# Cosine attention and a gated layer on one core: one quad's transposes, the order of the loads, one multiply, the last store, and the planner's transfer times

## Chip, core and metric

The kernel runs on one core of a Trainium2 chip. The metric is the device time of one execution in microseconds. It is measured in several runs, of which the median is given, and one further execution is recorded by the hardware profiler. All lines L... are lines of the kernel before.

## What is computed

For 8 batches and 12 heads, with 448 tokens and 64 elements a head, the rows of q and k are divided by their norms, and softmax(q k^T / 0.1) v is formed. The heads of a token then stand side by side, 768 wide, and pass through two dense layers with h cos(h) between them.

```python
q_n = q / (np.linalg.norm(q, axis=-1, keepdims=True) + 1e-06)
k_n = k / (np.linalg.norm(k, axis=-1, keepdims=True) + 1e-06)
scores = np.matmul(q_n, k_n.transpose(0, 1, 3, 2)) / tau          # tau = 0.1
attn = softmax(scores);  attn_out = np.matmul(attn, v)
x = attn_out.transpose(0, 2, 1, 3).reshape(B * S, H * D)          # 3584 x 768
h = x @ w_in                                                      # 768 x 2048
out = (h * np.cos(h)) @ w_out                                     # 2048 x 768
```

## The kernel before, in words

**Quads.** The work of the attention is cut into 24 quads of four heads, three for each batch (quad = 3 batch + 0, 1, 2). For a quad the kernel does the following.

- It loads q and k from DRAM as f32 into one of three buffers `Qf` and `Kf` (`load_qk`, L401, two DMAs issued by SyncE) and v into one of four (`load_v`, a DMA of GpSimd's queue).
- It squares them (`square`, L450, on GpSimd from quad 3 on) and sums the squares (L454, VectorE). Both stand in `norm_a`.
- It forms the inverse norms (`inverse`, L480 to L493, ScalarE and for some quads VectorE) and scales q and k to bf16 tiles `Qn` and `Kn` (`scale`, L501, GpSimd from quad 3 on). Both stand in `norm_b`.
- It transposes `Qn` and `Kn` to `qT` and `kT`. There are two ways. `transpose` (L516) lets TensorE transpose seven 128x128 blocks into a PSUM bank (L523), and VectorE copies the bank to `qT` or `kT` (L534); quads 0 to 2 use it. `turn` (L539) issues two DMA transposes on SyncE (L544); quads 3 to 23 use it.
- For each of seven steps it forms the scores (`scores`, L560, four matmuls), and ScalarE takes their exponential from two PSUM banks into a tile `E` (L567); `attend` (L577) multiplies `E` with v into banks 4 and 5. After the seventh step VectorE copies these banks to `AVs` (L586).
- It forms the sums of the softmax. For quads 0 to 2 this is done on the chip (`spread`, L599). From quad 3 on `sums` (L642) does it for one or two quads at a time: 14 matmuls a quad, a logarithm and an exponential on ScalarE (L649, L651), a DMA of the inverses to a DRAM tensor `rscr` issued by ScalarE (L652), two DMAs on SyncE for each quad that read them back, spread over the partitions, as `R` (L658), and a multiply of `AVs` with `R` into the bf16 tile `xT` (L661, GpSimd).

**Batches.** When the three quads of a batch are in `xT`, the first layer runs (`m1_part`, L675: 96 matmuls in eight pairs of blocks of 128), with the cosine behind it: two passes of ScalarE (L688, L692) and two of VectorE (L690, L694) for each pair, the last of which writes `gT`. The second layer (`m2`, L703) takes tiles of 128 tokens and the output's two halves of 384; each half is 16 matmuls. VectorE copies the half to `osb` (L711), and after the second half two DMAs on SyncE store the tile, 64 tokens each (L717).

**The order.** Quads 0 to 2 are done in a hand-written prologue. Then the loop over batches c = 0 to 7 does the first layer of batch c and interleaves the second layer of batch c with the quads that lie ahead: `QUADS = [5, 4, 3, 3, 3, 3, 0, 0]`, so quads 3 to 7 stand beside batch 0 and quads 8 to 11 beside batch 1. Before the first group of scores `fill(2 * E2)` puts 24 second-layer matmuls (L965). `group` (L745) takes two steps of a quad; at a quad's first step it calls `begin` (L739) and `norm_a` of the quad three ahead, and at its last step `turn` of the quad two ahead. `begin(qd)` loads q and k of quad qd + 4 and runs `norm_b` of quad qd + 2. Quad 3's turn is called right behind the prologue (L901).

**Engines and queues.** All instructions are objects of a `Planner` (class at the file's top). TensorE keeps the order in which the program made them. For ScalarE, VectorE, GpSimd and SyncE the planner simulates the run with the durations that each `op` is given, picks the next instruction of each engine by readiness and urgency, and so writes a fixed order for each engine before the run. A DMA is given the time `moves` that its transfer takes; `land` lets the transfers of a queue follow each other and slows them where two queues overlap. `lead` makes an instruction more urgent. Instructions made with `keep=True` keep their order among themselves on their engine. On SyncE these are the turns, and the loads of q and k of quads 5 and up; the loads of `R` and the stores are placed freely. At run time each engine works strictly in its order and waits for semaphores.

What a DMA issue looks like to the planner:

```python
o.lat = self.FIRST + moves + self.LAST if dma else self.LAT[eng]      # FIRST, LAST = 1.2, 0.8
```

## Time and profile before

| | |
|---|---|
| median of 3 runs | 444.45 us (443.76 to 445.1) |
| span of the profiled execution | 447.7 us; the page gives no other time for it |
| TensorE, matmul (PE) | 423.9 us busy, 95% of the span |
| ScalarE (ACT) | 315.3 us, 70% |
| VectorE (DVE) | 252.9 us, 56% |
| GpSimd (POOL) | 212.3 us, 47% |
| DMA queue of SyncE | 51.85 MB, 46.4% of 16 engines' span |
| DMA queue of GpSimd | 11.80 MB, 17.5% |

The profile is one execution, cut into instructions. A row of a timeline has the start, the length, the engine, the line, the operation, the tiles written and read, and in brackets the engine's idle time before it with the instruction that ended it. `PEld` is the load of weights into TensorE, which overlaps the matmuls. `SPq` is SyncE's own queue: issuing a DMA, not moving it. A row of the chain has start, length and what the end of the run was waiting for at that time. A row of stretches has the busy time of each engine, the clock granted to TensorE and the share in which the DMA engines were busy; the share can exceed 1 where packets of several queues overlap. Matmul records overlap by their pipelined ends, so the time of one matmul is read from a run of many.

### The profile page before, as it was taken

To read this page: it belongs to the slowest core of one execution; us is meant where nothing else is said; L and a number is where in the kernel's file an instruction comes from. 1 tells how busy PE (TensorE), PEld (TensorE's weight loads), DVE (VectorE), ACT (ScalarE), POOL (GpSimd) and SP (SyncE) were. 2 spreads that over 40 slices of the span, in tenths; PEclk is the share of its full clock that TensorE was granted. 3 is DMA by queue.
4 is the path that set the end of the run, shared out by engine and by line. 5 is a ranking of instruction groups with operands and counts; after the bars stand their busy time and mean duration, and the time that the engine had idled before them with its cause. 6 is when DMAs were issued, how large, how long until landed. Compare 5 with 4: busy or idle time off the path is not lost.

```text
span 447.7 us, 8380 instructions
## 1 busy us (share of the span) xinstructions
PE 423.9 (95%) x3530; PEld 206.4 (46%) x3530; DVE 252.9 (56%) x297; ACT 315.3 (70%) x434; POOL 212.3 (47%) x146
## 2 busy tenths in 40 slices
PE   7989978898999999999999999999999999999995
PEld 6444533233544445534454445534454445555553
DVE  4766974351894438935485348935484136825921
ACT  4898768785778887879678766879678666715700
POOL 3787618577628967069635682069232020030000
PEclk9999999988999999999999999999999999999999
DMA  7999998995917999159951996057811711051022
GB/s 248 237 256 222 221 233 106 272 205 139 252 23 152 265 182 253 29 132 250 171 154 39 240 210 170 1 130 191 164 38 35 162 40 34 0 156 35 1 70 72
DMA packets 72639, 64.81 MB, mean 145 GB/s; under 512 B 41924, under 2 KB 64792, under 8 KB 72600
## 3 DMA queue, kind: packets, MB, share of 16 engines
q1 hardware_dynamic: 59600, 51.85, 46.4%
q0 software_dynamic: 12288, 11.80, 17.5%
q8 instruction: 28, 0.46, 0.4%
q10 hardware_dynamic: 712, 0.61, 0.4%
q14 instruction: 11, 0.09, 0.1%
HBM read 55.25 MB, written 11.16 MB: 148 GB/s over the span
## 4 chain that ended last, share of the span: by engine, by line
PE 75%; DMA 13%; POOL 4%; ACT 3%; DVE 2%; issue 2%; SPq 1%; ACTq 0%; POOLq 0%
PE PS L703 30%; PE PS L675 29%; DMA Kf<-in_k_dram 8%; PE PS L560 6%; PE PS L577 5%; PE PS L642 3%; ACT E L567 2%; DMA kT<-Kn 2%; DMA R<-rscr 1%; DMA Qf<-in_q_dram 1%; POOL sqk L450 1%; DMA rscr<-Zs 1%; POOL Qn L501 1%; POOL Kn L501 1%; DVE n L454 1%
## 5 line engine op out<-in xcount | busy, mean ns | idle before, releaser
L567 ACT ACTIVATE E<-PS 128x896 bf16<-128x896 f32 x168 | 144.8, 916 | 30.3 <-PE PS L560 27.1
L703 PE MATMUL PS<-W,gT 128*128 128x384 bf16 x896 | 163.9, 328 | 1.8 <-DVE osb L711 1.0
L675 PE MATMUL PS<-xT,W 128*128 128x448 bf16 x768 | 149.2, 355 | 2.2 <-POOL xT L661 2.2
L703 PEld LDWEIGHTS PS<-W,gT 128*128 128x128 bf16 x896 | 80.2, 98 | 82.2 <-issue 28.8
L675 PEld LDWEIGHTS PS<-xT,W 128*128 128x128 bf16 x768 | 74.8, 98 | 73.9 <-issue 3.4
L688 ACT ACTIVATE ar<-PS 128x896 int32<-128x896 f32 x64 | 58.2, 911 | 51.1 <-PE PS L675 51.1
L690 DVE SCALAR_TENSOR_TENSOR ar<-ar,PS 128x896 f32<-128x896 int32 x64 | 69.2, 1083 | 32.2 <-ACT ar L688 32.2
L661 POOL TENSOR_TENSOR xT<-AVs,R 128x896 bf16<-128x896 f32 x21 | 43.5, 2085 | 87.8 <-DMA R<-rscr 87.8
L711 DVE COPY osb<-PS 128x384 f32<-128x384 f32 x56 | 30.2, 555 | 91.3 <-PE PS L703 91.3
L694 DVE TENSOR_TENSOR gT<-PS,ar 128x896 bf16<-128x896 f32 x64 | 69.6, 1088 | 1.5 <-ACT ar L692 1.0
L560 PE MATMUL PS<-qT,kT 64*64 64x448 bf16 x672 | 61.9, 367 | 8.7 <-DMA kT<-Kn 4.3
L692 ACT ACTIVATE ar<-ar 128x896 f32<-128x896 f32 x64 | 60.6, 946 | 12.9 <-DVE ar L690 12.9
L450 POOL TENSOR_TENSOR sqq<-Qf 128x896 bf16<-128x896 f32 x21 | 35.3, 1681 | 56.8 <-DVE n L454 36.8
L577 PE MATMUL PS<-E,Vb 64*64 64x448 bf16 x672 | 50.8, 354 | 1.6 <-ACT E L567 1.4
L450 POOL TENSOR_TENSOR sqk<-Kf 128x896 bf16<-128x896 f32 (+1 forms) x22 | 36.7, 1669 | 22.9 <-DVE n L454 12.9
L501 POOL TENSOR_TENSOR Qn<-Qf,rr 128x896 bf16<-128x896 f32 x21 | 35.5, 1690 | 14.6 <-ACT rr L493 14.5
L586 DVE COPY AVs<-PS 128x896 f32<-128x896 f32 x21 | 22.9, 1091 | 31.1 <-PE PS L577 31.1
L560 PEld LDWEIGHTS PS<-qT,kT 64*64 64x64 bf16 x672 | 18.6, 105 | 42.4 <-ACT E L567 15.8
L501 POOL TENSOR_TENSOR Kn<-Kf,rr 128x896 bf16<-128x896 f32 (+1 forms) x22 | 36.7, 1669 | 0.5 <-DVE Qn L501 0.5
L454 DVE TENSOR_REDUCE n<-sqk 128x14 f32<-128x896 bf16 (+2 forms) x24 | 25.0, 1040 | 8.0 <-POOL sqk L450 7.9
L454 DVE TENSOR_REDUCE n<-sqq 128x14 f32<-128x896 bf16 (+2 forms) x24 | 25.0, 1041 | 5.0 <-POOL sqq L450 4.5
L577 PEld LDWEIGHTS PS<-E,Vb 64*64 64x64 bf16 x672 | 19.4, 106 | 17.6 <-ACT E L567 10.5
(51 smaller groups left out, 174.1 us busy)
## 6 DMA issues: line engine op xcount, KB each, us to landing
Qf<-in_q_dram SPq DMA_DIRECT2D x24, 448.0 KB, 5.3
out_dram<-osb SPq DMA_DIRECT2D x56, 192.0 KB, 2.9
Kf<-in_k_dram SPq DMA_DIRECT2D x23, 448.0 KB, 5.9
R<-rscr SPq DMA_DIRECT2D x42, 224.0 KB, 4.6
Vb<-in_v_dram POOLq DMA_DIRECT2D x24, 224.0 KB, 5.6
W<-in_moe_w_in_dram POOLq DMA_DIRECT2D x4, 768.0 KB, 17.1
W<-in_moe_w_out_dram POOLq DMA_DIRECT2D x4, 768.0 KB, 29.7
qT<-Qn SPq DMA_TRANSPOSE x21, 4.5
```

The lines of the kernel that those rows point to most:

```text
L450: op(eng, (1.68 if eng == "pool" else 1.05) * n, lambda e: e.tensor_tensor(dst, src, src, ALU.mult), r=cut(nm + "f", s, part), w=at, after ...
L454: return op("dve", 0.07 + 0.95 * n, lambda e: e.tensor_reduce(out=n2[u].ap()[:, H * w:H * w + H] if part == ALL[0] else jr(n2[u], w, part) ...
L501: lambda e: e.tensor_tensor(n[u].ap()[:, j0:j1].rearrange("p j r d -> p r j d"), f[s].ap()[:, :, j0:j1], rb, ALU.mult),
L560: ins = e.matmul(bank(bs + r, S, 64 * a, 64 * a + 64), kT[u].ap()[64 * r:64 * r + 64, j, a, :], qT[u].ap()[64 * r:64 * r + 64, :, a, :], s ...
L567: act("exp", 0.875, lambda e: e.activation(E[es].ap(), two(bs), ACT.Exp, bias=0.0, scale=INV_TAU), r=pair(bs), w=[("E", es)], chain="E")
L577: ins = e.matmul(bank((X, Y)[a], S, 64 * r, 64 * r + 64), Vb[vs].ap()[64 * a:64 * a + 64, r, j, :], E[es].ap()[64 * a:64 * a + 64, r, :], ...
L675: ins = e.matmul(bank(bk + i2), W1.ap()[:, i, 128 * nb:128 * nb + 128], xT[c % 2].ap()[:, i, :], start=(i == 0), stop=(i == NKC - 1))
L688: op("act", 0.815, lambda e: e.activation(ar[s].ap().bitcast(I32), two(bk), ACT.Identity, bias=0.25, scale=INV2PI), r=bs, w=[("ar", s)])
L690: op("dve", 1.005, lambda e: e.scalar_tensor_tensor(ar[s].ap(), ar[s].ap().bitcast(I32), -2.0 * math.pi, two(bk), ALU.mult, ALU.add), r=bs ...
L692: act("sin", 0.86, lambda e: e.activation(ar[s].ap(), ar[s].ap(), ACT.Sin, bias=GUARD * math.pi / 2.0, scale=GUARD), r=[("ar", s)], w=[("a ...
L694: op("dve", 1.01, lambda e: e.tensor_tensor(gT.ap()[:, 2 * pr:2 * pr + 2, col:col + S], two(bk), ar[s].ap(), ALU.mult), r=bs + [("ar", s)] ...
L703: ins = e.matmul(bank(bk, HW), gT.ap()[:, f, col:col + 128], W2.ap()[:, f, HW * h:HW * h + HW], start=(f == 0), stop=(f == NNB - 1))
```

## The change

It has five parts.

- Quad 3 is transposed by TensorE. The call of `turn(FIRST)` behind the prologue goes; behind the first layer of batch 0 two calls of `transpose` come, into banks `free` and `free + 1` (2 and 3). In batch 0 the fill ahead of the first scores is 2 x E1 = 20 matmuls instead of 2 x E2 = 24.
- The loads of q and k of quad qd + 4 are made behind `turn(qd + 2)` at the quad's last step and no longer in `begin(qd)`. This holds for quads 8 to 23.
- The multiply that gives quad 5's x (the last of batch 1) is made on VectorE instead of GpSimd.
- The last output tile is stored in halves: each half of 384 columns gets its two DMAs as soon as it is copied, and of the second half one is issued by ScalarE.
- The transfer times that the planner is given are changed.

```diff
 load_one:    moves=0.17 * (j1 - j0)   ->  moves=0.196 * (j1 - j0)
 load_v:      moves=1.41  ->  1.67
 load_w1:     moves=4.15  ->  4.26
 load_w2:     moves=4.32  ->  5.18
 turn:        moves=1.2   ->  1.61
 R (L658):    moves=0.82  ->  0.85
 store (L717): moves=0.64 ->  0.66
@@ sums
-            op("pool", 2.04, lambda e, u=u, sl=sl, b=b, c0=c0: e.tensor_tensor(
+            late = qd == 2 * QB - 1
+            op("dve" if late else "pool", 1.02 if late else 2.04, lambda e, u=u, sl=sl, b=b, c0=c0: e.tensor_tensor(
                 xT[b % 2].ap()[:, c0:c0 + 2, :], AVs[sl].ap(), R[u].ap(), ALU.mult),
@@ m2
-        if f1 == NNB:
+        if f1 == NNB and t == B * S // 128 - 1:
+            so = t % 3
+            op("dve", 0.475, lambda e: e.tensor_copy(osb[so].ap()[:, HW * h:HW * h + HW], bank(bk, HW)),
+               r=whole(bk), w=[("o", so, h)])
+            for sg, eng in enumerate(("sp", "act" if h else "sp")):
+                b, cc = divmod(128 * t + 64 * sg, S)
+                dst = bass.AP(out.tensor, (S * b + cc // 64) * KM + HW * h, [[NJ * KM, 64], [1, HW]])
+                op(eng, 0.5, lambda e, sg=sg, dst=dst: e.dma_start(
+                    dst, osb[so].ap()[64 * sg:64 * sg + 64, HW * h:HW * h + HW]),
+                   r=[("o", so, h)], w=[("out", t, sg, h)], dma=("store", t, h, sg), moves=0.32)
+        elif f1 == NNB:
@@ begin
-        if FIRST < qd < NQ - 4:
-            load_qk(qd + 4)
         if FIRST < qd < NQ - 2:
             norm_b(qd + 2, after=[o for o in P.ops if o.chain][-1:])
@@ group
         if qd + 2 < NQ and j == NJ - 1:
             turn(qd + 2)
+            if FIRST < qd < NQ - 4:
+                load_qk(qd + 4)
@@ behind the prologue
     load_qk(FIRST + 3)
-    turn(FIRST)
     norm_b(FIRST + 1, after=ended[-1:])
@@ loop over batches, behind the first layer
         if c == 0:
+            transpose(FIRST, 0, free)
+            transpose(FIRST, 1, free + 1)
             norm_a(FIRST + 2, [o for o in P.ops if o.eng == "dve"][-1:])
@@
         if todo:
-            fill(2 * E2)
+            fill(2 * (E2 if c else E1))
```

More of the change, by code (lines that the diff above doesn't have):

```diff
@@ L398, in load_one @@
         return op(eng, 0.5, lambda e: e.dma_start(dst[s].ap()[:, :, j0:j1].rearrange("p r j d -> p r (j d)"), ap),
-                  w=cut(nm, s, part), dma=(nm, s, j0), moves=0.17 * (j1 - j0), after=after, keep=qd > 4)
+                  w=cut(nm, s, part), dma=(nm, s, j0), moves=0.196 * (j1 - j0), after=after, keep=qd > 4)
     def load_qk(qd, after=()):
@@ L410, in load_v @@
         return pool_dma(0.75, lambda e: e.dma_start(Vb[s].ap().rearrange("p r j d -> p r (j d)"), ap),
-                  w=[("V", s)], dma=("V", s), moves=1.41, after=after)
+                  w=[("V", s)], dma=("V", s), moves=1.67, after=after)
     NW = 2
@@ L717, in m2 @@
                     op("sp", 0.5, lambda e, sg=sg, dst=dst: e.dma_start(dst, osb[so].ap()[64 * sg:64 * sg + 64, :]),
-                       r=[("o", so, 0), ("o", so, 1)], w=[("out", t, sg)], dma=("store", so, sg), moves=0.64)
+                       r=[("o", so, 0), ("o", so, 1)], w=[("out", t, sg)], dma=("store", so, sg), moves=0.66)
     QUADS = [5, 4, 3, 3, 3, 3, 0, 0]
```

8 lines of the change are left out of this document (4 added, 4 removed).

## The prediction

> **What bounds the kernel now.** I read the page's first part, then a table of stretches, then the waits and the chain between 36 and 112 us. The first row is of the page, the others of the table of stretches (columns: stretch, length, busy time of PE, PEld, DVE, ACT, POOL, granted clock, DMA share, GB/s).
>
> ```profile
> span 447.7 us, 8380 instructions
> ```
> ```profile
> 57.00:63.50 6.50, 4.07 (x24) 2.27 (x24) 5.26 (x5) 3.19 (x4) 0.00 (x0) 1.00 1.26 203
> ```
> ```profile
> 86.10:88.00 1.90, 0.00 (x0) 0.00 (x0) 0.00 (x0) 0.00 (x0) 1.90 (x2) 1.00 0.97 331
> 88.00:103.70 15.70, 15.30 (x164) 5.07 (x164) 6.99 (x7) 13.48 (x24) 10.39 (x8) 0.89 0.95 232
> 103.70:105.80 2.10, 0.00 (x0) 0.00 (x0) 0.56 (x1) 1.93 (x2) 2.10 (x2) 1.00 0.41 131
> 105.80:112.20 6.40, 6.37 (x28) 2.79 (x28) 1.09 (x1) 0.92 (x1) 6.40 (x4) 0.73 0.36 83
> ```
> ```profile
> 110.00:442.60 332.60, 329.65 (x2612) 161.56 (x2610) 189.35 (x205) 232.27 (x310) 142.51 (x90) 1.00 0.53 122
> ```
>
> From 110 us to the last matmul TensorE is idle for 332.60 - 329.65 = 2.95 us. It takes its instructions in program order there and is the bound; nothing that only rearranges the other engines can win more than those 2.95 us in that part. What can be won lies before 110 us and behind the last matmul. Before 110 us there are holes in TensorE's row, at 61 to 63.5, 86.1 to 88 and 103.7 to 105.8, and behind the last two the granted clock is 0.89 and 0.73. The chain of waits says what each hole waits for.
>
> ```profile
> 75.60 4.84 DMA Qf<-in_q_dram
> 80.44 7.52 DMA kT<-Kn
> ...
> 97.47 6.17 DMA R<-rscr
> 103.64 0.07 issue
> 103.70 2.08 POOL xT L661
> ```
>
> Quad 6's scores wait until 88 us for its transposed keys, and these stand in SyncE's queue behind the load of quad 8 (the Qf row at 75.60; the keys landed at 80.44 + 7.52 = 87.96). The first matmul of batch 1 waits for quad 4's scaled x, at the end of a path by DRAM (the sums' inverses are written there and read back as R). The first hole is quad 3's transpose, in the timelines of TensorE and SyncE; the last row is the DMA view of that SyncE issue alone, with its time to landing.
>
> ```profile
> 57.03 3.26 PE L703 MATMUL PS<-W,gT 128*128 128x384 bf16 x19 [0.86 <-DVE gT L694]
> ```
> ```profile
> 63.51 0.57 PE L560 MATMUL PS<-qT,kT 64*64 64x448 bf16 x8 [2.41 <-DMA kT<-Kn]
> ```
> ```profile
> 47.41 5.73 SPq L544 DMA_TRANSPOSE kT<-Kn  x1
> ```
> ```profile
> kT<-Kn SPq DMA_TRANSPOSE x1, 16.1
> ```
>
> The transpose was issued at 47.41, took 5.73 us to get into the queue and landed 16.1 us after its issue, at 63.5, behind weights that keep the DMA engines at a share of 1.26.
>
> **The change part by part.** *Quad 3 by TensorE.* It adds 14 transposes and two copies and takes two DMA transposes away; 20 second-layer matmuls instead of 24 stand ahead of the first scores. The costs are in these rows of TensorE, VectorE and ScalarE.
>
> ```profile
> 25.92 0.56 PE L523 MATMUL PS<-ident,Qn 128*128 128x128 bf16 x7 [0.32 <-DVE Qn L501]
> ```
> ```profile
> 26.78 0.62 DVE L534 COPY qT<-PS 128x896 bf16<-128x896 bf16 x1
> ```
> ```profile
> 57.16 1.09 DVE L690 SCALAR_TENSOR_TENSOR ar<-ar,PS 128x896 f32<-128x896 int32 x1 [0.18 <-ACT ar L688]
> ```
> ```profile
> 59.25 1.28 ACT L371 ACT_TABLE_LOAD   x1
> 63.95 1.73 ACT L567 ACTIVATE E<-PS 128x896 bf16<-128x896 f32 x2 [3.42 <-PE PS L560]
> ```
>
> Two runs of seven transposes take some 2 x 0.5 = 1.0 us, from 57.03 - 0.86 = 56.2 (the last first-layer matmul) to 57.2. Of that 0.86 us is the idle time that TensorE has there anyway; without that cover the full 1.0 us would count. Then 20 matmuls, at the 0.163 us that 3.26 us for 19 come to less the pipelined end of one, last to 60.5, and the scores need no DMA. The two copies are new on VectorE: 2 x 0.55 us, and queued behind them are the last L690 and two L694. If they go first, L690 starts at 58.0 instead of 57.16, and L692 and the table load (59.25 + 1.28 = 60.5) end 0.85 us later, at 61.4; the exponentials then start at 61.4 instead of 63.95. This is 2.6 us; if the copies go behind L690, table load ends at 60.5 and scores at 60.9: 3.0 us. At the other end stands 0, worked out under the rivals. I take 2.6, nearest to the rows.
>
> *The loads of q and k behind the turns.* The group that issued load 8 and then turn 6 (the transposes of quad 6) issues them the other way about, and so does every later one.
>
> ```profile
> 76.12 1.69 POOL L501 TENSOR_TENSOR Kn<-Kf,rr 128x896 bf16<-128x896 f32 x1
> ```
> ```profile
> kT<-Kn SPq DMA_TRANSPOSE x21, 4.3
> ```
>
> Kn of quad 6 is done at 77.8, so its turn could be issued at 77.8 instead of 80.44, and with nothing large ahead land in the median 4.3 us, at 82.1, instead of 87.96. Everything up to there also moves by the 2.6 us of the first part. The scores of quad 6 would ask for it at 86.1 - 2.6 = 83.5 against a landing at 79.5: 4 us in hand. The hole of 1.93 us goes, and so does what the lowered clock cost in the softmax sums behind it:
>
> ```profile
> 88.77 2.27 PE PS L642 x28
> ```
> ```profile
> 132.91 1.47 PE PS L642 x28
> ```
>
> That is 2.27 - 1.47 = 0.8 us, so 2.7 us in all; bounds 0 (the wait returns) and 2.7. What is late next is load 8 itself, some 3 us behind. Its squares are not needed before batch 1's groups at 130 us, but GpSimd has a fixed order in which they may stand ahead of something urgent; that is in the rivals. The next loads, 9, 10 and so on, slip behind turn 7, turn 8 likewise. The R loads aren't tied to that chain; one load of q and k fewer lies between 75 and 105 us.
>
> *Quad 5's x on VectorE.* GpSimd's L661 takes 2.08 us twice in a row, for quads 4 and 5. Batch 1's first eight matmuls need quads 3 and 4 only, so what ends that wait is quad 4's multiply, still on GpSimd, still 2.08 us behind R. The move removes only a second, short wait of the weight loads (total, times, longest):
>
> ```profile
> PEld PS L675 <- POOL xT L661: 2.8, 2, 2.5
> ```
>
> 2.8 - 2.5 = 0.3 us. On VectorE the same shape costs 1.09 us (L690's row), in a stretch where VectorE is busy 0.56 of 2.10 us. The multiply waits for R, and behind it VectorE would hold an output copy and batch 1's first L690, which both need batch 1 anyway or come 2 us later. The path from the sums to x is as long as before, so both it and TensorE's work move up by the same 2.6 + 2.7 us and the wait of 2.16 us stays, less what R gains from the load that is missing:
>
> ```profile
> R<-rscr SPq DMA_DIRECT2D x42, 224.0 KB, 4.6
> ```
>
> R took 6.17 us there, 4.6 in the median of the kernel: 0 to 1.6 us, of which I take 1.0, as the DMA share of 0.95 leaves most of the crowd in place. The clock behind it is the last term: the 24 first-layer matmuls at 105.83 took 6.40 us, and later
>
> ```profile
> 165.68 4.54 PE PS L675 x24
> ```
>
> so 1.86 us more is to be had only if the wait goes. I take 0 of it. This part: 0.3 + 1.0 = 1.3 us, bounds 0 and 2.16 + 0.3 + 1.86 = 4.3.
>
> A page speaks against this move. The Trainium skill, "SBUF — State Buffer", section "Who interferes with whom", says that a VectorE instruction with both inputs in SBUF and a GpSimd instruction that reads SBUF exclude each other for their whole length. No row of this trace shows the two side by side. It is the second rival.
>
> *The last tile in halves.*
>
> ```profile
> 442.65 0.56 DVE L711 COPY osb<-PS 128x384 f32<-128x384 f32 x1 [2.04 <-PE PS L703]
> 443.23 1.79 SPq L717 DMA_DIRECT2D out_dram<-osb  x2
> ```
> ```profile
> out_dram<-osb SPq DMA_DIRECT2D x2, 192.0 KB, 3.1
> ```
>
> Two issues in 1.79 us from one queue become one on SyncE and one on ScalarE, which is idle there, and each moves half the bytes. At most one issue, 0.9 us, goes; the 3.1 us to landing were for 192 KB and may stay nearly whole. I take 0.6, bounds 0.3 and 0.9.
>
> *The planner's numbers.* They change no instruction, only the order on ScalarE, VectorE, GpSimd and SyncE. I cost that at 0, between a gain of 2.95 us (all idle time behind 110 us) and a loss that the rivals bound.
>
> **The sum**: 2.6 + 2.7 + 1.3 + 0.6 = 7.2 us, so a span of 447.7 - 7.2 = 440.5. The page gives no time beside that span, which is 3.25 us above the median of the runs, 444.45; I take the same difference off the median: 437.2.
>
> **The rivals.** *The wait moves to quad 4* (439.8). Its scores come seven groups behind quad 3's, and this row of the weight loads shows that its keys landed just then:
>
> ```profile
> 70.56 0.11 PEld L560 LDWEIGHTS PS<-qT,kT 64*64 64x64 bf16 x4 [0.32 <-DMA kT<-Kn]
> ```
>
> If they still land at 70.5, all 2.6 us of the start are lost again: 444.45 - 4.6 = 439.8. For it: the DMA engines are full until 70 us. Against it: the transposes of quad 3 were ahead of them in the queue, and a pair of them fills the engines for 4 x 0.86 = 3.4 us, as one alone shows:
>
> ```profile
> 347.00:351.00 4.00, 4.00 (x53) 1.89 (x52) 1.29 (x2) 2.79 (x4) 0.00 (x0) 1.00 0.86 119
> ```
>
> 3.4 us earlier is more than the 2.6 that is asked. Chance 0.15.
>
> *VectorE's multiply holds up GpSimd's* (438.3). If the two can't overlap and VectorE comes first, quad 4's x is 1.09 us later and 437.2 becomes 438.3; if GpSimd is first, quad 5's is done at 105.78 + 1.09 = 106.9 instead of 107.8 and nothing is lost. Chance 0.05.
>
> *Loads too late in every stage* (449.6): the slower side. From quad 8 on each load waits for a turn, which waits for GpSimd, which must square that load before the turn after next. Place: the group stages of batches 1 to 5.
>
> ```profile
> 140.83 1.31 SPq L544 DMA_TRANSPOSE kT<-Kn  x1
> ```
> ```profile
> 148.46 0.38 PE L560 MATMUL PS<-qT,kT 64*64 64x448 bf16 x4
> ```
> ```profile
> 135.00:140.00 5.00, 5.00 (x56) 2.06 (x49) 0.56 (x1) 4.43 (x6) 5.00 (x4) 1.00 0.32 99
> ```
>
> Quad 10's turn is issued at 140.83 and, at 4.3 us, lands at 145.1, 3.3 us ahead of its scores; GpSimd is busy 5.00 of 5.00 us there, so squares that are pushed into that stretch push the turn. Three squares at the 1.69 us of a scaling of the same shape (the Kn row), moved behind 131 us, would make 5.0 us, a wait of 1.7 us, and with 0.8 us of lowered clock 2.5 us. Once, this leaves the change faster; in all five stages it is 12.4 us and the time is 444.45 - 7.2 + 12.4 = 449.6. It decides from 7.2 / 5 = 1.4 us a stage. Against it: from batch 2 on there are three quads in a stage and not four, and the turns come during the first layer, well ahead. The replanned order can reach the same place by another engine's head of queue, so I give 0.23.
>
> *The holes only move* (444.7): the replan gives back the start, say with quad 6's squares or quad 7's turn behind a late load on GpSimd, and the x path still ends where it did, at 105.8. For it: GpSimd's order is fixed ahead of the run by the planner's times, and every square in it waits for its load. Then 0.6 us of the tail is left against the 0.85 us by which VectorE's copies delay the first layer's end: 444.45 - 0.6 + 0.85 = 444.7. Chance 0.07.
>
> **How the numbers follow.** Forecast 0.50, its own range 434.0 to 439.5. A measurement of this kernel can tell about 0.3%, 1.3 us, from no change. Faster: 0.50 + 0.15 + 0.05 = 0.70; within: 0.07; slower: 0.23. For the range I take the forecast down to 433.5 (x's 4.3 instead of 1.3 and the tail's 0.9 are 433.9) and go up past the holes that move to 447.0, into the weaker part of the slower case; above lies most of the 0.23.
>
> **What would show it.** Exponentials of quad 3 from about 61.4 us; no wait of L560 for a kT from DMA at quads 4 and 6; first-layer matmuls of batch 1 at about 99 instead of 105.8 us, still after a wait for L661; the stretch from there to the last matmul as long as now within 3 us; the last store one issue shorter. I am wrong if that later stretch grows, with L560 waiting for kT in batches 1 to 5, or if a wait at quad 4 or 7 eats the start.

## The result and the profile after

| | before | after |
|---|---|---|
| median of 13 runs, same chip | 443.48 us (442.38 to 450.26) | 441.97 us (440.57 to 442.81) |
| ratio, 95% interval | | 0.9947 (0.9923 to 0.997) |
| span of the profiled execution | 447.7 us | 439.6 us |

The change wins 1.5 us by the medians, a fifth of the 7.2 that I forecast. By the ratio it is 0.53%, 2.4 us, and the interval, 0.23 to 0.77% (1.0 to 3.4 us), leaves out no change. The ratio is not the quotient of the two medians, which is 0.9966; in the runs below the two ways differ by up to 1 us. The two spans say 8.1 us, because the profiled execution of before was one of its long ones: in all runs here the time is 1.6 to 2.9 us above the span, 1.8 in the median, so that execution took some 449.5 us, which 4 of 158 executions of the kernel before reach (449.46 to 451.11). So the kernel before was profiled again (run e1, below) and that span is 441.3. First rows of the two pages, e1 and then after:

```profile
span 441.3 us, 8380 instructions
```
```profile
span 439.6 us, 8369 instructions
```

Against e1 the difference is 1.7 us, and this table says where it comes from (times in us from the start of the span, read from TensorE's timeline):

| | profiled before | e1 | after | after, stage by stage against e1 |
|---|---|---|---|---|
| first layer of batch 0 starts | 37.84 | 39.69 | 38.64 | -1.05 |
| scores of quad 3 | 63.51 | 64.57 | 61.19 | -2.33 |
| softmax sums of quads 4, 5 | 88.70 | 87.77 | 84.66 | +0.27 |
| first layer of batch 1 | 105.83 | 101.77 | 100.28 | +1.62 |
| last matmul ends | 442.61 | 436.87 | 435.68 | +0.30 |
| end of the span | 447.7 | 441.3 | 439.6 | -0.51 |

The first row is no work of the change: up to there the engines' orders in e1 and after are the same, and that start lies between 37.3 and 39.7 us in the eighteen profiles. What the change did is 2.33 us won by quad 3, 0.51 at the tail, and 1.62 lost between the softmax sums and batch 1. All rows without the first come to 0.65 us, less than the 1.5 or 2.4 of the timed runs; two profiles don't tell more closely than that.

TensorE at quad 3, e1 and after (start, length, what it is, in brackets the idle time before it and what ended that):

```profile
64.57 0.57 PE L560 MATMUL PS<-qT,kT 64*64 64x448 bf16 x8 [1.61 <-DMA kT<-Kn]
```
```profile
57.84 3.42 PE L704 MATMUL PS<-W,gT 128*128 128x384 bf16 x20
61.19 0.57 PE L560 MATMUL PS<-qT,kT 64*64 64x448 bf16 x8
...
100.28 4.71 PE L676 MATMUL PS<-xT,W 128*128 128x448 bf16 x24 [1.18 <-POOL xT L662]
```

The scores follow the 20 matmuls without a gap. The last row is batch 1's first layer, which now waits 1.18 us for quad 4's x; in e1 it starts without a wait. The same stretch, from the softmax sums to batch 1, as a stretch of each of the three profiles (before, e1, after; columns as in the prediction):

```profile
88.70:105.83 17.13, 14.61 (x156) 4.81 (x153) 7.48 (x8) 15.15 (x25) 11.81 (x10) 0.90 0.88 212
```
```profile
87.77:101.77 14.00, 12.88 (x156) 4.54 (x153) 6.92 (x7) 13.03 (x24) 12.82 (x10) 1.00 1.00 239
```
```profile
84.66:100.28 15.62, 12.86 (x156) 4.45 (x153) 7.99 (x9) 13.38 (x24) 11.10 (x8) 1.00 0.99 207
```

TensorE's work in it is 12.9 us at the full clock in e1 and after; in the profiled execution of before it was 14.61 us, at a clock of 0.90. What after lost to e1 is idle time: 15.62 - 12.86 = 2.76 us against 1.12.

Two things end ahead of that wait, half a microsecond apart: the path by DRAM and GpSimd's own order. First the path. In the queues of ScalarE (L652 writes the inverses of the sums) and SyncE (L398 loads q and k, L658 reads R back), e1:

```profile
90.51 0.57 ACTq L652 DMA_DIRECT2D rscr<-Zs  x1
```
```profile
91.18 0.88 SPq L398 DMA_DIRECT2D Qf<-in_q_dram  x1
92.10 0.47 SPq L398 DMA_DIRECT2D Kf<-in_k_dram  x1
92.86 0.48 SPq L658 DMA_DIRECT2D R<-rscr  x1
```

and after:

```profile
87.40 0.57 ACTq L652 DMA_DIRECT2D rscr<-Zs  x1
```
```profile
85.83 0.63 SPq L398 DMA_DIRECT2D Qf<-in_q_dram  x1
86.51 1.22 SPq L398 DMA_DIRECT2D Kf<-in_k_dram  x1
93.28 2.86 SPq L658 DMA_DIRECT2D R<-rscr  x4
```

R waits for the store of 14 KB: 92.86 - 90.51 = 2.35 us in e1, where the load (quad 10's) was issued behind the store, and 93.28 - 87.40 = 5.88 us in after, where the load (quad 9's) is 1.57 us ahead of it. Part of that is made up again by a quicker R: quad 4's R has landed 8.3 us behind the store's issue in e1 and 10.2 in after (issued at 93.81, 3.8 us to landing, so at 97.6). Then GpSimd, e1 and after:

```profile
98.84 2.08 POOL L661 TENSOR_TENSOR xT<-AVs,R 128x896 bf16<-128x896 f32 x1 [0.98 <-DMA R<-rscr]
```
```profile
93.22 1.69 POOL L501 TENSOR_TENSOR Qn<-Qf,rr 128x896 bf16<-128x896 f32 x1 [4.30 <-ACT rr L493]
94.87 1.68 POOL L450 TENSOR_TENSOR sqq<-Qf 128x896 bf16<-128x896 f32 x1
96.51 1.68 POOL L450 TENSOR_TENSOR sqk<-Kf 128x896 bf16<-128x896 f32 x1
98.15 2.08 POOL L662 TENSOR_TENSOR xT<-AVs,R 128x896 bf16<-128x896 f32 x1
```

In e1 GpSimd waits for R. In after it doesn't: R is there at 97.6, and GpSimd's order has a scaling and the two squares of load 9 ahead of the multiply, until 98.19. The scaling came late itself, behind 4.30 us of waiting for ScalarE's inverse norms. So the order ends last, by 0.5 us: a quicker path alone would not have shortened the wait of 1.18 us, and another order alone by no more than that 0.5 us, as long as R comes when it does. From the first of the sums to the end of quad 4's multiply it is 13.15 us in e1 and 15.57 in after; 2.0 of the 2.4 are the later R, the rest is the order.

The tail, after (VectorE, ScalarE's queue, the DMA view):

```profile
435.71 0.56 DVE L712 COPY osb<-PS 128x384 f32<-128x384 f32 x1 [2.04 <-PE PS L704]
```
```profile
436.30 0.53 ACTq L717 DMA_DIRECT2D out_dram<-osb  x1
```
```profile
out_dram<-osb SPq DMA_DIRECT2D x3, 96.0 KB, 2.1
out_dram<-osb ACTq DMA_DIRECT2D x1, 96.0 KB, 2.4
```

From the last matmul to the end it is 3.92 us, and was 4.43 in e1.

### The profile page after: what moved, and what is told of

It reads as the page before. It is cut to its first block, busy times and chain, and to the rows that moved or that the text cites. A ratio compares the mean times of both kernels' runs of the same rounds, so it can differ in the third digit from the quotient of the medians.

```text
span 439.6 us, 8369 instructions
## 1 busy us (share of the span) xinstructions
PE 420.1 (96%) x3544; PEld 204.6 (47%) x3544; DVE 254.7 (58%) x300; ACT 315.3 (72%) x434; POOL 211.2 (48%) x145
## 4 chain that ended last, share of the span: by engine, by line
PE 83%; ACT 9%; DVE 3%; issue 2%; POOL 2%; ACTq 1%; POOLq 0%
PE PS L676 33%; PE PS L704 31%; PE PS L560 7%; PE PS L577 6%; ACT E L567 6%; PE PS L642 4%; DVE n L454 1%; ACT Zs L651 1%; ACT Zs L649 1%; ACTq L652 1%; PE PS L599 1%; PE PS L623 1%; POOL xT L662 0%; DVE gT L695 0%; ACT ar L609 0%
## 5 line engine op out<-in xcount | busy, mean ns | idle before, releaser
L676 PE MATMUL PS<-xT,W 128*128 128x448 bf16 x768 | 147.7, 353 | 1.2 <-POOL xT L662 1.2
L691 DVE SCALAR_TENSOR_TENSOR ar<-ar,PS 128x896 f32<-128x896 int32 x64 | 69.2, 1083 | 29.0 <-ACT ar L689 29.0
L722 DVE COPY osb<-PS 128x384 f32<-128x384 f32 x54 | 29.2, 554 | 86.6 <-PE PS L704 86.5
L662 POOL TENSOR_TENSOR xT<-AVs,R 128x896 bf16<-128x896 f32 x20 | 41.4, 2088 | 67.5 <-DMA R<-rscr 67.4
L695 DVE TENSOR_TENSOR gT<-PS,ar 128x896 bf16<-128x896 f32 x64 | 69.6, 1088 | 1.5 <-ACT ar L693 1.0
```

Source lines behind the costliest of these rows:

```text
L676: ins = e.matmul(bank(bk + i2), W1.ap()[:, i, 128 * nb:128 * nb + 128], xT[c % 2].ap()[:, i, :], start=(i == 0), stop=(i == NKC - 1))
L691: op("dve", 1.005, lambda e: e.scalar_tensor_tensor(ar[s].ap(), ar[s].ap().bitcast(I32), -2.0 * math.pi, two(bk), ALU.mult, ALU.add), r=bs ...
L695: op("dve", 1.01, lambda e: e.tensor_tensor(gT.ap()[:, 2 * pr:2 * pr + 2, col:col + S], two(bk), ar[s].ap(), ALU.mult), r=bs + [("ar", s)] ...
```

## The experiments

Times are medians. Each run stands beside runs of the kernel before on the same chip, and the ratio is to these. The kernel before has a median of 443.48 to 443.73 us beside after, e1 to e4 and e9 to e12, and of 444.64 or 444.83 beside e5 to e8 and e13 to e16, on another chip. So two runs are compared by what each of them is above or below the kernel before beside it, by the medians and, in brackets, by the ratios.

**Which profile stands for the kernel before?** e1 is that kernel with no edit.

> The kernel before, unchanged, profiled anew. Theory one (an odd execution): the profiled execution of before, with its span of 447.7 us, was one of a rare slow kind, and the usual one has neither the wait of 1.93 us for quad 6's transposes nor the lowered clock behind it and in the first layer of batch 1; the new profile has a span of 440.5 to 442.5 us, and of the three holes only the one for quad 3 (2.4 us) is there in full. Theory two (the profile stretches it): a profiled execution of before always has these waits and a timed one does not; the new span is 446 to 449 us with the same three holes.

443.26 us against 443.67, ratio 0.9993 (0.9963 to 1.0023); span 441.3. Of the holes on which my sum rested, 2.41 us for quad 3's keys, 1.93 for quad 6's and 2.16 for x, only the first is there, as 1.61. 2.7 + 1.3 = 4.0 us of the forecast were in the one profiled execution and not in the usual one. Theory one came, but for the hole of quad 3, which is not there in full.

**The parts one by one, on the kernel before.** e2 is quad 3 alone:

```diff
@@ behind the prologue
-    turn(FIRST)
@@ behind the first layer of batch 0
+            transpose(FIRST, 0, free)
+            transpose(FIRST, 1, free + 1)
@@ ahead of the first scores
-            fill(2 * E2)
+            fill(2 * (E2 if c else E1))
```

> The kernel before with quad 3 transposed by TensorE and the shorter fill, nothing else. Theory one: the start of the exponentials moves up by 2.3 to 2.6 us, and as hardly any other hole is there in the usual execution, this is nearly all that the whole change wins: 440.9 to 441.6 us against 443.5. Theory two: the same 2.6 us against a time that holds all the holes, so also 441 us, but the profile keeps a wait of about 2 us for quad 6's transposes and a slowed clock.

442.69 against 443.67, ratio 0.9974 (0.9944 to 1.0004): 1.0 us won by the medians, and the interval touches no change. In its profile the scores of quad 3 stand 22.55 us behind the first layer's start, as in after (e1: 24.88), so 2.33 us are won there. 1.46 of them are given back by the softmax sums of quads 4 and 5, which stand 24.66 us behind these scores (e1: 23.20). The time that both theories expected, 440.9 to 441.6 us, was missed.

e3 is the loads alone, and e13 is the same kernel once more:

```diff
@@ begin
-        if FIRST < qd < NQ - 4:
-            load_qk(qd + 4)
@@ group
             turn(qd + 2)
+            if FIRST < qd < NQ - 4:
+                load_qk(qd + 4)
```

> The kernel before with the loads of q and k issued behind the turns, nothing else. Theory one: the wait that this removes is not in the usual execution, so the time stays within 0.7 us of 443.5. Theory two: 2.7 us faster, 440.8 us.

> The kernel before with the loads of q and k behind the turns and nothing else, a second time: it was 2.9 us slower than the kernel before, but the profile had caught its fastest execution. Theory (the keys of quads 4 to 7 are late in the usual execution): L560 waits for a kT from DMA at quads 3 and 4 together for over 2.7 us, and the stretch from batch 1's first matmul to the last is no longer than before's 335 us by more than 0.5. Rival (the loads come too late in the later stages, my slower rival): L560 or L675 waits in batches 1 to 5, and that stretch is 336.5 to 338 us. Time 445.5 to 447, span 443.5 to 445.

e3: 446.36 against 443.67, ratio 1.0065 (1.0042 to 1.0087). e13: 446.62 against 444.83, 1.0039 (1.0002 to 1.0075). The move alone makes the kernel slower, by 2.7 and 1.8 us (2.9 and 1.7); neither of e3's theories allowed for that. The profile of e3 caught its fastest execution (443.46), that of e13 a usual one (446.5). In e13, TensorE:

```profile
86.89 0.38 PE L560 MATMUL PS<-qT,kT 64*64 64x448 bf16 x4 [0.81 <-DMA kT<-Kn]
...
98.93 0.57 PE L577 MATMUL PS<-E,Vb 64*64 64x448 bf16 x8 [1.89 <-DVE AVs L586]
```

SyncE's queue, VectorE and two stretches behind the second wait:

```profile
78.38 1.17 SPq L658 DMA_DIRECT2D R<-rscr  x2
79.64 1.26 SPq L544 DMA_TRANSPOSE qT<-Qn  x1
80.94 1.34 SPq L544 DMA_TRANSPOSE kT<-Kn  x1
82.33 1.27 SPq L398 DMA_DIRECT2D Qf<-in_q_dram  x1
```
```profile
96.79 1.09 DVE L454 TENSOR_REDUCE n<-sqq 128x14 f32<-128x896 bf16 x1 [2.29 <-POOL sqq L450]
97.79 1.08 DVE L586 COPY AVs<-PS 128x896 f32<-128x896 f32 x1
```
```profile
100.00:102.00 2.00, 2.00 (x19) 0.58 (x18) 0.00 (x0) 1.74 (x3) 2.00 (x2) 0.60 1.06 267
102.00:104.00 2.00, 2.00 (x16) 0.56 (x15) 0.00 (x0) 1.97 (x8) 2.00 (x2) 0.55 0.14 23
```

Three things are to be seen. Load 8 does stand behind quad 6's turn, but the turn is issued no earlier for it: 80.94 us here, 80.44 in the profiled execution of before. What stands ahead of it in SyncE's queue is R, which waits 3.3 us there for the store of its inverses. Second, VectorE has the sum of a late load's squares in its order ahead of the copy of quad 5's AV, and waits 2.29 us for GpSimd with the copy behind it; TensorE waits 1.89 us for the copy. In e1 the copy goes first (at 96.06) and there is no such wait. Third, that hole is followed by a clock of 0.60 and 0.55. The stretch from the sums to batch 1 is 16.88 us instead of 14.00, 2.9 us longer; from batch 1 to the last matmul it is 335.98 us against e1's 335.10. So neither of e13's expectations came: the waits for keys are 1.26 us at quad 3 (e1: 1.61) and 0.81 at quad 6, and the later stages lose 0.9 us and not the 1.4 to 3 of the rival. The late load costs once, ahead of batch 1.

e4 is the last tile in halves alone, the edit of `m2` shown above.

> The kernel before with the last tile stored in halves, nothing else. Both theories: the end behind the last matmul gets 0.3 to 0.9 us shorter, 442.6 to 443.2 us against 443.5.

442.87 against 443.67, ratio 0.9996 (0.9963 to 1.0028): within the 442.6 to 443.2 expected, and not told apart from no change. In its profile the end comes 3.62 us behind the last matmul, against 4.43 in e1.

**The changed kernel without one part.** e8 leaves the loads where they were:

```diff
@@ begin
+        if FIRST < qd < NQ - 4:
+            load_qk(qd + 4)
@@ group
-            if FIRST < qd < NQ - 4:
-                load_qk(qd + 4)
```

> The changed kernel with the loads of q and k where they were before. Theory one: the move of the loads is what gives back most of the start, since it puts a load just ahead of the small store; without it the store lands in 2 to 3 us, and the time is 0.5 to 1.2 us under the changed kernel's 442.0. The reason on record in the prediction: the move is worth 2.7 us, so without it 444.7 us.

446.62 against 444.64, ratio 1.0041 (1.0019 to 1.0063): 2.0 us above before where after is 1.5 below, so 3.5 us slower than after (4.2), though the same move alone lost 1.8 to 2.7. Theory one had the sign wrong; the prediction's 2.7 had it right, though neither of the holes that it was made of is there. e9 leaves out x on VectorE as well (`late` goes):

> The changed kernel with the loads where they were and quad 5's multiply back on GpSimd: quad 3 by TensorE, the last tile in halves and the planner's new times are left. Theory three (VectorE shut out): in the run without the loads' move quad 5's multiply took 4.21 us on VectorE, because its two inputs in SBUF could not be read while GpSimd went from one multiply to the next; TensorE waited 2.55 us for it. On GpSimd it takes 2.08 us behind quad 4's, TensorE waits at most 0.6 us, and the time falls by 2 to 3 us, from 446.6 to 443.6 to 444.6. Rival (the late loads' order as such): what made that run slow is where GpSimd and ScalarE got their work, and the time stays at 446 to 447 us.

445.17 against 443.73, ratio 1.0024 (1.0005 to 1.0044): between the two expectations. TensorE's waits are as theory three has them, 0.59 and 0.34 us, and the span of e9's profile is 2.2 us under e8's, but it caught a quicker execution than usual (444.26). By the times e9 is 0.5 us under e8 (0.8) and the intervals overlap, so that the move of x to VectorE is a loss in that order is seen in the profiles and not shown by the times. In after's profile there is no wait for quad 5's x, and e14 asks what makes the difference. It is e8 with one wait more: GpSimd's two scalings behind its multiply wait for VectorE's.

```diff
@@ begin, behind norm_b(qd + 2)
+            if qd == FIRST + 4:
+                for o in P.ops[-2:]:
+                    o.deps = sorted({*o.deps, P.last_write["x", 1, 2].i})
```

> The kernel after without the loads' move, in which VectorE's multiply for quad 5 lasted 4.21 us (alone 1.09) beside two scalings of GpSimd that followed each other; here these two scalings wait for that multiply, nothing else is changed. Theory (the two engines shut each other out): the multiply lasts 1.1 to 1.5 us, TensorE waits under 1 us for it instead of 2.55, and the time is 1.5 to 3 us under the 446.6 of the run without this wait. Rival (the multiply was long for its R that came late, or for TensorE's or the DMA's traffic): it stays at 3 to 4.2 us and the time within 0.7 us of 446.6.

443.84 against 444.83, ratio 0.9956 (0.9929 to 0.9984), so 3.0 us under e8 (3.8), on the same chip, as the theory has it. VectorE, GpSimd and TensorE of e8:

```profile
103.17 4.21 DVE L662 TENSOR_TENSOR xT<-AVs,R 128x896 bf16<-128x896 f32 x1
```
```profile
101.06 2.08 POOL L662 TENSOR_TENSOR xT<-AVs,R 128x896 bf16<-128x896 f32 x1
103.10 1.68 POOL L501 TENSOR_TENSOR Qn<-Qf,rr 128x896 bf16<-128x896 f32 x1
104.75 1.68 POOL L501 TENSOR_TENSOR Kn<-Kf,rr 128x896 bf16<-128x896 f32 x1
```
```profile
107.43 3.20 PE L676 MATMUL PS<-xT,W 128*128 128x448 bf16 x16 [2.55 <-DVE xT L662]
```

and of e14, VectorE and GpSimd:

```profile
103.34 1.08 DVE L662 TENSOR_TENSOR xT<-AVs,R 128x896 bf16<-128x896 f32 x1
```
```profile
104.50 1.69 POOL L501 TENSOR_TENSOR Qn<-Qf,rr 128x896 bf16<-128x896 f32 x1 [1.19 <-DVE xT L662]
106.15 1.69 POOL L501 TENSOR_TENSOR Kn<-Kf,rr 128x896 bf16<-128x896 f32 x1
```

Beside GpSimd's two scalings, one right behind the other until 106.43, VectorE's multiply took 4.21 us and ended 0.95 us after them; without them it took 1.08, and TensorE's wait of 2.55 us is gone. This is shown: GpSimd shuts VectorE out. That it also goes the other way is seen in after, where GpSimd's scaling beside VectorE's multiply took 2.53 us instead of 1.68; in e10, without that multiply, it takes 1.69. The remainder between e14 and after, 0.5 us (0.4), is then what the loads' move is worth in the whole once VectorE is no longer shut out, and it can't be told from nothing. By the two profiles it is 2.5 us, in the same stretch as ever. In e14 that is 18.48 us long, at a clock of 0.91; TensorE waits twice for exponentials:

```profile
88.19 0.38 PE L560 MATMUL PS<-qT,kT 64*64 64x448 bf16 x4 [1.19 <-ACT E L567]
...
91.60 0.38 PE L560 MATMUL PS<-qT,kT 64*64 64x448 bf16 x4 [1.45 <-ACT E L567]
```

e10 puts quad 5's x back on GpSimd in the changed kernel, e11 gives the planner its old transfer times, e12 turns quad 3 by DMA again (`turn(FIRST)` back, no `transpose`, `fill(2 * E2)`).

> The changed kernel with quad 5's multiply back on GpSimd. Theory three: in the changed kernel the multiply was shut out for only 0.34 us (1.43 instead of 1.09) and GpSimd's next scaling for 0.85 us (2.53 instead of 1.68), so the move gains or loses little: quad 5's x is done at 98.15 + 2 x 2.08 = 102.3 instead of 101.2, TensorE asks for it 1.5 us behind 100.28, and the time is 0.2 to 0.7 us above the changed kernel's 442.0. The step of the prediction (0.3 us) lies in that range. If a replan dominates, it differs by more than 1 us either way.

442.88 against 443.73, ratio 0.9964 (0.9941 to 0.9987): 0.7 us slower than after (0.8), as theory three expects, but the intervals overlap.

> The changed kernel with the planner's old transfer times. The prediction had this part at 0, within a gain of 2.95 us. If the orders that the planner picks decide as much as the runs so far suggest (the loads' move alone cost 2.9 us, and beside the other parts saved 4.6), it differs from the changed kernel by 1 us or more; if they were noise, it stays within 0.7 us of 442.0.

440.95 against 443.73, ratio 0.9948 (0.9918 to 0.9977): the lowest median of all, 1.3 us under after against before, but its ratio is after's. The new times win nothing that can be told, and neither of the two expectations is settled. In its order the store of the inverses is issued at 87.49 and load 9 at 87.56, and R follows the store by 2.65 us.

> The changed kernel with quad 3 back on the DMA transpose and 24 matmuls ahead of the first scores. The step of the prediction: 2.6 us of start are lost, 444.6 us. Theory one: of the start most was given back at batch 1's first layer, where the changed kernel waits 1.2 us for x, so only 0.5 to 1.5 us are lost, 442.5 to 443.5 us. If the transposes that come back also crowd the DMA engines ahead of quad 4's, it is slower than 444.6 us and the profile has a wait of quad 4's scores for kT.

448.16 against 443.73, ratio 1.0093 (1.0059 to 1.0126), from four runs: 5.9 us slower than after (6.5), where quad 3 is worth 2.3 at its own place. The third expectation came, with the wait for quad 4's keys. TensorE:

```profile
62.25 0.57 PE L560 MATMUL PS<-qT,kT 64*64 64x448 bf16 x8 [1.71 <-DMA kT<-Kn]
70.95 0.38 PE L560 MATMUL PS<-qT,kT 64*64 64x448 bf16 x4 [1.58 <-DMA kT<-Kn]
105.42 6.40 PE L676 MATMUL PS<-xT,W 128*128 128x448 bf16 x24 [3.59 <-POOL xT L662]
```

With quad 3 back on the DMA quad 4's keys are late too, and GpSimd's order has two scalings and two squares ahead of quad 4's multiply, which begins at 103.29 us without idle time although its R had landed at 99.6. 24 matmuls behind that hole took 6.40 us against 4.71 in after.

**Load 9 and the store of the inverses.** In e5 load 9 waits for the store, in e15 (and in e16, with the planner's old times) until quad 4's multiply; in e6 quad 4's multiply is on VectorE too, and e7 is e5 with e6.

```diff
@@ e5
-                load_qk(qd + 4)
+                loads[qd + 4] = load_qk(qd + 4)
@@ behind the sums of quads 4 and 5
+                    if rounds[0] == 2:
+                        for o in loads[FIRST + 6]:
+                            o.deps = sorted({*o.deps, P.last_write["rs", 1].i})
@@ e15, e16: the last line
+                            o.deps = sorted({*o.deps, P.last_write["x", 1, 1].i})
@@ e6
-            late = qd == 2 * QB - 1
+            late = QB < qd < 2 * QB
```

> The changed kernel, but the load of quad 9, which now is issued 1.6 us ahead of the store of the softmax inverses for quads 4 and 5, waits until that store has landed. Theory one (a load ahead of a small store): the store waits behind the load in the DMA engines, 5.9 us from its issue to SyncE's next step where it took 2.4 us when it came first; with the load held this falls to 2.0 to 3.0 us, quad 4's x is ready 3 us earlier, the wait of 1.2 us at batch 1's first matmul goes, and the time falls by 0.8 to 1.2 us against the changed kernel's 442.0. Theory two (GpSimd's order): quad 4's x is late because it stands behind two squares on GpSimd; the store may land sooner but the first layer of batch 1 starts no earlier, and the time stays at 441.5 to 442.5 us.

> The changed kernel with quad 4's multiply on VectorE as well as quad 5's. Both theories let the multiply be 1.0 us shorter (1.09 instead of 2.08 us). Theory one: R is what it waits for, so the wait of 1.2 us shrinks to about 0.2 us and the time falls by 0.7 to 1.1 us. Theory two: it also no longer stands behind GpSimd's squares, so the wait goes in full and R is seen to have landed more than 1 us before.

> Both edits in one. Theory one and two alike: the first layer of batch 1 then starts when TensorE has done its second-layer matmuls, no later than with the load held alone; 0.8 to 1.4 us faster than the changed kernel, 440.6 to 441.2 us. If it is no faster than the changed kernel, the wait for x was never worth its length, and something behind it (the table load of ScalarE, 0.9 us behind the first matmul) takes its place.

> The kernel after, in which load 9 (q and k of quad 9) waits for quad 4's multiply, so that it shares the DMA engines neither with the store of the inverses nor with R. When it waited for the store alone, the time from the softmax sums to quad 4's x went from 15.58 to 14.05 us at the store, and R became longer. Theory (load 9 is a third of what the path by DRAM lost): from the end of the sums to the end of quad 4's multiply 12.5 to 13.6 us (13.15 in the usual execution of before), batch 1's first matmul 1.5 to 2.5 us earlier than the 100.28 of the kernel after; time 439.5 to 441 if load 9 is early enough for its squares, up to 444 if not. Rival (the path is set by turn 7, the loads of v and the queue's own latency): the path stays at 14.5 us or more and the time at 441.5 to 443.

> The same wait of load 9 for quad 4's multiply in the kernel after with the planner's old transfer times, the quickest version so far (440.95). There the store of the inverses went out just ahead of load 9 and the time from the sums' end to quad 4's x was already short, so the first theory expects 0 to 0.7 us of gain (440.2 to 441.2), and a loss of up to 2 us if load 9 comes too late for its squares. The rival expects no change within 0.5 us.

All times in this table but the first are of the one profiled execution, whose own time is in the second column. "R landed" is quad 4's; the last column is how long the engine of quad 4's multiply sat idle for it, and 0 means that the engine's own order ended later.

| | time, ratio (interval) | profiled | store's issue to R's issue | store's issue to R landed | first of the sums to end of quad 4's multiply | idle for R |
|---|---|---|---|---|---|---|
| e1 | 443.26, 0.9993 (0.9963 to 1.0023) | 443.11 | 2.35 | 8.3 | 13.15 | 0.98 |
| after | 441.97, 0.9947 (0.9923 to 0.997) | 441.8 | 5.88 | 10.2 | 15.57 | 0 |
| e5 | 444.09, 0.9981 (0.9948 to 1.0014) | 445.6 | 4.61 | 10.0 | 14.86 | 0.20 |
| e6 | 442.23, 0.9952 (0.9929 to 0.9975) | 443.18 | 5.95 | 11.0 | 16.13 | 0 |
| e7 | 442.71, 0.9961 (0.9936 to 0.9986) | 443.5 | 4.53 | 9.0 | 12.85 | 2.38 |
| e11 | 440.95, 0.9948 (0.9918 to 0.9977) | 441.09 | 2.65 | 9.8 | 14.64 | 1.02 |
| e15 | 447.28, 1.0057 (1.0026 to 1.0088) | 444.72 | 3.86 | 9.8 | 14.71 | 0 |
| e16 | 444.13, 0.9972 (0.9945 to 1.0) | 445.92 | 2.96 | 9.9 | 14.79 | 3.46 |

With load 9 out of its way R is issued 1.3 to 2.0 us sooner behind the store in e5, e7 and e15 than in after; with the planner's old times (e16 against e11) it is not. But R's own transfer becomes longer: in e5 and e15 it has landed only 0.2 to 0.5 us sooner, and the path wins 0.7 and 0.9 us of the 2.4 that after lost to e1. e15's expectation of 13.6 us or less missed, and its rival's 14.5 or more was met. e7 against e6 is the exception: there the held load is worth 2.0 us to R and 3.3 to the path. So load 9 has a share of the loss, and how much of it depends on the order that the planner makes of the rest.

What the wait for x is worth is seen in e7. There it is gone, and e7 is no quicker than after: TensorE waits 1.47 us for a copy of AV and 0.88 for gT in the first layer of batch 1 instead, since VectorE has the sums of load 9's squares in its order ahead of them. That is the case which e7's last sentence names. In e6 the wait became longer, 1.74 us, as the multiply now stands behind such a sum on VectorE; both of its theories missed. None of the versions that hold load 9 is quicker than after by more than can be told, and e15 is slower by 4.0 us (4.9); the times expected of e5, e7 and e15 were missed. e16 is 2.1 us slower than e11 (1.1), which its theory allows where load 9 comes too late. The profile of e15 caught the fastest of its twelve executions and that of e16 the slowest, so their rows stand for these executions. TensorE and VectorE of e15:

```profile
112.35 9.25 PE L676 MATMUL PS<-xT,W 128*128 128x448 bf16 x48 [3.00 <-DVE gT L695]
```
```profile
98.35 2.15 DVE L662 TENSOR_TENSOR xT<-AVs,R 128x896 bf16<-128x896 f32 x1 [4.13 <-DMA R<-rscr]
```

VectorE had the sums of load 9's squares in its order ahead of gT, and from batch 1 to batch 2 it is 61.62 us instead of after's 58.10. No version tried beats the changed kernel by more than the measurement can tell.

## Why the prediction was wrong, step by step

- **The base.** "The page gives no time beside that span, which is 3.25 us above the median" and "I take the same difference off the median": this is the step that failed first. In all runs here a span lies 1.6 to 2.9 us below its time; one that lies 3.25 above the median belongs to an execution some 5 us longer than usual, and the holes that I summed were that execution's. Two of the three holes are not in e1, and behind each of these two the clock was lowered for 3.4 us, which cost another 1.7 us each (last section). The warning stood in the sentence itself.
- **Quad 6's wait, 2.7 us: not there.** The usual execution has no wait for its keys (e1). And the cause was misread: "its turn could be issued at 77.8 instead of 80.44" overlooks R's issue between load 8 and the turn in SyncE's queue. With load 8 behind it the turn was issued at 80.94 (e13). The 0.8 us of lowered clock in the sums were in that execution alone: the 28 sums take 1.51 us in all other profiles.
- **Quad 5's x and R, 1.3 us: a loss.** "The path from the sums to x is as long as before" fell: it became 2.42 us longer, and TensorE waits 1.18 us for x. "Still 2.08 us behind R" fell too: R had landed 0.5 us before the multiply could start, and load 9's squares stood ahead of it on GpSimd. e1 has no wait for x, so there was nothing to win.
- **Quad 3 by TensorE, 2.6 us: the mechanism right**, 2.33, and the size in part by luck. The copies went behind the last L691 and one L695, which is the case that I had priced at 3.0, and the usual hole is 1.61 us and not 2.41; the two nearly cancel. That the exponentials start at 61.63 us where I had written 61.4 holds the later start of the first layer as well. **The tail, 0.6: right**, 0.51 in after and 0.81 in e4's profile. **The planner's numbers, 0: right** as far as can be told (e11).
- **The rivals.** *The wait moves to quad 4* did not come, and the argument against it holds: a wait for quad 4's keys is there in two of the runs that move the loads and leave quad 3 on the DMA (0.96 us in e3, 1.58 in e12; not in e13, where quad 6's keys are late), and in none where TensorE transposes quad 3. *VectorE's multiply holds up GpSimd's*: the mechanism is shown, the direction and price were wrong. I had GpSimd 1.09 us late, and nothing lost if GpSimd is first; in e8 GpSimd was first and VectorE was shut out for 4.21 - 1.09 = 3.1 us. In after it is 1.43 us for the multiply and 2.53 instead of 1.68 for the scaling behind it, and TensorE waits for neither. The Trainium skill, "SBUF — State Buffer", section "Who interferes with whom", has this as an exclusive lock that goes to whoever issues first; the runs agree but for one case: in e8 GpSimd kept it over two scalings in a row, though VectorE had been waiting since the first. In after and e6 VectorE came in between two instructions of GpSimd that follow each other; what decides this stays open. I had written that no row of before's trace shows the two side by side, and overlooked one: at 7.52 us a square of GpSimd, 128x640, takes 1.46 us beside a scaling of VectorE, while GpSimd's scaling of that shape takes 1.25 at 11.06. *Loads too late* came as "another engine's head of queue", on VectorE and at one place each, around the first layer of batch 1, in e3, e13, e5, e7, e15 and e16. Nearest to it in after are load 9's squares on GpSimd ahead of quad 4's x; no later wait of TensorE there is over 1 us. *The holes only move* is nearest to what happened: a part of the start is given back by the x path (1.62 of 2.33 us), but not all of it, and the tail stays.

The sizes that I added up as if they were independent are not. The loads' move loses 1.8 to 2.7 us alone (e13, e3) and wins 3.5 within the whole (e8), of which 3.0 are the lock (e14); quad 3 is worth 1.0 us alone and 5.9 within the whole (e2, e12). x on VectorE is not told from nothing in either order (e8 and e9, e10). Each edit makes the planner lay out four engines' orders anew, and my sum has no term for that.

**What stays open**: why the path from the store's issue to the end of quad 4's multiply still needs 12 us with load 9 held away (e15, e16) and 10.4 in e1. Quad 7's turn and the loads of v are still beside them and were not tried alone. Nor was a kernel tried in which GpSimd does quad 4's multiply ahead of load 9's squares and the loads stay as they are in after, which would part its order from the path.

## What to carry to other kernels

Before a sum is made of the holes of one profile, put its span beside the timed runs: if it doesn't fit the median, those holes are that execution's own, and a second profile is worth more than any argument. In a queue that keeps its order, name what stands directly ahead of the late instruction: moving something that stands further ahead moves nothing. And where a planner lays out the orders anew, take the value of an edit only from the kernel in which it will stand.

## What the runs showed of the hardware

- A short hole of TensorE can cost as much again in the clock. From batch 0's first layer to the last matmul, a lowered clock is 0.50 for 3.41 us in each of the six profiles that have one, and 1.00 on either side. Before (twice) and e14, as stretches with these ends:

```profile
89.24:92.65 3.41, 3.41 (x35) 1.16 (x27) 1.11 (x2) 2.05 (x4) 3.41 (x3) 0.50 0.88 171
106.31:109.72 3.41, 3.41 (x11) 1.38 (x10) 0.00 (x0) 0.00 (x0) 3.41 (x3) 0.50 0.19 59
```
```profile
89.58:92.99 3.41, 1.73 (x20) 0.49 (x21) 1.16 (x2) 2.76 (x4) 3.41 (x4) 1.00 1.00 305
92.99:96.41 3.42, 3.42 (x22) 0.96 (x26) 1.48 (x2) 2.36 (x5) 2.25 (x2) 0.50 0.32 83
```

  The two stretches of before start 17.07 us apart, which is five times 3.41, and e14's clock is lowered again at 441.15, 348.16 us or 102 times 3.41 behind the first: the clock goes by windows of a fixed grid. The Trainium skill, "TensorE: Matmul & The Clock Gate", "Part 1: The HAM clock gate", tells of a free-running window of about 3.4 us; the traces agree. A hole that lies whole in one window can lower the next: e14's wait of 1.45 us, from 90.15 to 91.60, and before's of 1.93 (86.08 to 88.01) and 2.16 (103.67 to 105.83) do. Each lowered window with work throughout costs 1.7 us: 24 first-layer matmuls took 6.40 us in the second one of before and 4.70 in e1. e8's wait of 2.55 us, from 104.88 to 107.43, falls into two windows (one starts at 92.91, where e8's lowered clock begins, and the fourth after it at 106.57) and doesn't:

```profile
103.15:106.57 3.42, 1.69 (x8) 0.70 (x8) 3.42 (x2) 0.96 (x1) 3.27 (x2) 1.00 1.14 338
106.57:109.98 3.41, 2.55 (x14) 1.36 (x15) 1.43 (x2) 0.92 (x1) 0.00 (x0) 1.00 1.12 357
109.98:113.40 3.42, 3.42 (x22) 1.57 (x21) 2.86 (x4) 2.04 (x3) 2.12 (x2) 1.00 0.99 290
```

  So length alone doesn't decide, and e15's wait of 3.00 us was not followed by a lowered clock either. Idle time in one window doesn't decide alone: e6's wait of 1.74 us and e16's of 1.82 lower nothing, and by the grid each lies whole in one window. It would fit that executions of one kernel differ by some 2 to 6 us, as the same hole can fall into one window or into two: before's reach 447 us or more in 17 of the 146 timed beside other kernels, after's 13 stay within 2.3 us. That is argued.
- A store of 14 KB, issued by another engine than the loads, takes 2.35 us until the next step when it is ahead of two loads of 448 KB (e1) and 5.88 behind them (after). With no such load near it, it still took 3.86 to 4.61 (e5, e7, e15), so the loads are not all of it.
- VectorE's multiply of 1.09 us takes 1.23 (e11) to 4.21 us (e8) where GpSimd works beside it. It ends about 1.0 us after the GpSimd instructions that shut it out do (e8, e11, e15).
